# A neural codec's encoder and quantizer on one core: four residual buffers with shared code columns, exponentials in dead buffers, strict silu phases, and a fixed list that orders all operations

## The chip, the core and the metric

The kernel runs on one core of one Trainium2 chip. Five engines work side by side, each through its own stream of instructions, and wait for one another by semaphores: TensorE (PE; its weight loads are listed apart as PEld), VectorE (DVE), ScalarE (ACT), GpSimd (POOL) and SyncE (SP, which here only issues DMAs). The metric is device time in microseconds, the median of the runs. Beside it stands one profiled execution, from which every duration below is taken.

## The reference

`x` is 2 x 16000 x 512 in bf16. A depthwise convolution over time with three taps, a silu, four rounds of residual vector quantization with eight code words each, and a second depthwise convolution of the summed code words:

```python
xp = jnp.pad(x, ((0,0),(pad,pad),(0,0)))
z = jnp.zeros_like(x)
for i in range(K):                       # K = 3
    z = z + xp[:, i:i+T, :] * dw_enc[i][None, None, :]
z = _silu(z)
res = z
q = jnp.zeros_like(z)
for s in range(Nq):                      # Nq = 4, C = 8 words each
    cb = codebooks[s]
    d2 = (res . res)[..., None] - 2.0 * (res . cb) + (cb . cb)[None, None, :]   # in bf16
    idx = d2.argmin(-1)
    sel = cb[idx]
    q = q + sel
    res = res - sel
...                                      # y: q convolved with dw_dec, three taps
```

## The kernel before, in words

Time is cut into 250 groups of 128 time steps (one per partition), and these into 17 chunks of 4, 12, 14 times 16, and 10 groups. A chunk passes through three parts.

- *Front* (`load`, `front`). DMA transposes bring `x` into `XT`, channels on partitions. For each of four blocks of 128 channels (`block(i)`): three products on DVE with the taps (`product`, L486, into a Z and two T buffers), two additions (`total`; by DMA with accumulation, L497, issued from POOL, or on DVE, L500/L502, the last one into the residual buffer RES), then silu as exponential on ACT (L508, into an E buffer), plus one on DVE (L512), reciprocal on ACT (L184), and a product on DVE (`silu`, L518). Exponential and reciprocal need different tables on ACT, and a change of table is an `ACT_TABLE_LOAD`.
- *Four rounds* (`stage`). `score` (L584, L590): PE multiplies each 64-step half of a group with itself and with the code words; the code words stand as extra columns inside RES. `lone` (ACT, L601) keeps the diagonal, `dots` (DVE, L620) copies the code columns, `total` (PE, L604, L611) adds the diagonal to them, `sums` (DVE, L616) brings the result to SBUF as VT. POOL then does `ties` (L645, L647), `distance` (L658) and `key` (L662), DVE the minimum (L666) and the one-hot (L672), POOL a copy of that (`note`, L678). PE and ACT turn the one-hot into a selection (L715 to L737), PE multiplies it with pairs of code words (L749), and DVE subtracts them from RES (`update`, L755, four per round; it reads PSUM). After the fourth round there is no update.
- *Decoder* (`finish`, `outputs`). PE multiplies the one-hots with tap-weighted code words (L773), ACT copies them to YSB (L779), SP stores them.

The rounds of one chunk are a chain across PE, ACT, DVE and POOL, so chunks are worked on side by side. There are three RES buffers, taken at a chunk's first write to RES and given back after its last scoring, four Z, four T and four E buffers, and four PSUM tiles of two banks. `Plan` collects all operations as tasks with an engine, a hold, a delay, needs, buffers and a due time (a table `START` by chunk plus `OFF` by operation). When the program is built, `Plan.run` plays this through and on each engine emits the ready task with the earliest due time. Where PE would stand idle in that play, it emits dummy matmuls (`warm`, L387; 129 in all). The order on each engine is fixed from then on; on the chip only the semaphores act.

Of the kernel before, what the change touches and what calls it, by code (L numbers as in the profile page):

```python
# [20 lines left out]
LC = 16  # L21
ROOM = 2 * GC + 2

SIZES = [4, 12] + [16] * 14 + [10]
# [5 lines left out]
WARM = 0.4  # L30
SPLIT = (1, 1, 1, 2)
RELU = (0, 1, 2, 3)

ZB, TB, EB, YB = 4, 4, 4, 2
# [3 lines left out]
START = [-49.78, -21.21, -11.1, 40.29, 77.41, 126.87, 171, 213.64, 259.89, 295.9, 339.35, 382.88, 414.63, 449.59, 490.48, 512.46, 542.77]  # L38
OFF = {
    "words": -209.08, "codes": -112.52, "col0": -187, "sums": -87.73, "mask": -228.88, "norms": -202.91, "col1": 18.74,  # L40
# [19 lines left out]
}  # L60


class Plan:

    def __init__(self, slots):
        self.slots = dict(slots)
        self.tasks = []
        self.names = []
        self.idle = None

    def add(self, engine, hold, delay, needs, due, emit, take=(), give=(), use=1.0):
        self.names.append(due)
        due = START[due[0]] + OFF[due[1]]
        self.tasks.append((engine, hold, delay, [n for n in needs if n is not None], due, emit, take, give, use))
        return len(self.tasks) - 1

    def run(self):
        tasks = self.tasks
        left = [len(t[3]) for t in tasks]
        after = [[] for _ in tasks]  # L80
        for n, t in enumerate(tasks):
            for d in t[3]:
                after[d].append(n)
        engines = list(dict.fromkeys(t[0] for t in tasks))
        ready = {e: [] for e in engines}
        until = {e: 0.0 for e in engines}
        spans = []
        for n, t in enumerate(tasks):
            if not left[n]:
                heapq.heappush(ready[t[0]], (t[4], n))  # L90
        now, events, order = 0.0, [], []
        while len(order) < len(tasks):
            going = True
            while going:
                going = False
                for e in engines:
                    if until[e] > now + 1e-9:
                        continue
                    passed, pick = [], None
# [46 lines left out]
def kernel(  # L146
# [235 lines left out]
    def warm():  # L382
        if not scored[2:]:
            return False
# [488 lines left out]
```

## Time and profile before

| what | value |
|---|---|
| median of 3 runs | 815.28 us (812.22 to 817.3) |
| profiled execution, its own time | 809.59 us |
| its span, first to last instruction | 807.8 us |
| mean granted TensorE clock | 0.897 |
| DMA: moved, mean rate | 107.71 MB, 133 GB/s |

The span is what the trace covers; the time holds a little more. A view of groups has one row for each line, engine, operation and shape: number, busy time and mean duration, then the idle time of the engine just before such instructions and what ended most of it. Busy times join overlapping instructions; single durations overlap somewhat with the next one's. A view of stretches gives, for each stretch of the span, the busy time of PE, PEld, DVE, ACT and POOL (with the number of instructions), the granted clock, the busy share of the DMA engines and GB/s. A view of waits gives engine and line, what it waited for, the time in total, how often and the longest. The view of one line gives minimum, median and maximum of its durations in ns. The chain of waits follows the work that ended last back to the start.

### The profile page before, as it was taken

How to read it: one execution, taken by the hardware profiler on the slowest of the kernel's cores; microseconds unless marked ns; L12 is line 12 of the kernel's file. 1: busy time of each engine (PE TensorE's matmuls, PEld its weight loads, DVE VectorE, ACT ScalarE, POOL GpSimd, SP SyncE). 2: the span in 40 equal slices, each digit the busy share in tenths (PEclk: the TensorE clock that was granted, in tenths of full speed). 3: DMA queues.
4: the chain of work that ended last, by engine and by line, in shares of the span. 5: the costliest groups of instructions: out<-in, count | busy, mean ns of one | idle time of the engine just before them, and what ended most of it. 6: DMA issues, size and time to landing. Idle time of an engine off the chain costs nothing.

```text
span 807.8 us, 28980 instructions
## 1 busy us (share of the span) xinstructions
PE 622.8 (77%) x13019; PEld 381.0 (47%) x13092; DVE 628.2 (78%) x1027; ACT 538.6 (67%) x571; POOL 284.9 (35%) x459
## 2 busy tenths in 40 slices
PE   3065787877878878887799877878885759889985
PEld 3023454544444544535356545554553526446543
DVE  5998889896988798878778897887969785855530
ACT  2345748494789477697847976866937596793553
POOL 1244353442534155426243452253414342212200
PEclk9568788999989999989999998998998979989989
DMA  4749677767796777895967778768984542121231
GB/s 150 112 83 153 130 133 134 124 121 164 141 207 147 164 145 175 136 176 117 166 153 121 203 139 184 128 140 153 187 158 68 105 121 93 47 92 44 80 157 79
DMA packets 149542, 107.71 MB, mean 133 GB/s; under 512 B 130217, under 2 KB 131370, under 8 KB 149290
## 3 DMA queue, kind: packets, MB, share of 16 engines
q1 hardware_dynamic: 137796, 66.62, 37.4%
q0 software_dynamic: 11472, 39.10, 27.0%
q8 instruction: 102, 1.67, 0.9%
q14 instruction: 22, 0.18, 0.1%
q10 hardware_dynamic: 150, 0.13, 0.1%
HBM read 3.70 MB, written 32.77 MB: 45 GB/s over the span
## 4 chain that ended last, share of the span: by engine, by line
PE 28%; DVE 19%; ACT 14%; issue 8%; POOL 7%; DMA 3%; ACTq 0%; another core or an unknown queue 0%; DVEq 0%; POOLq 0%
PE PS L590 12%; DVE RES L755 10%; PE PS L749 5%; ACT YSB L779 4%; PE PS L584 4%; ACT E L184 3%; PE PS L773 3%; PE PS L611 2%; ACT E L508 2%; POOL S L645 2%; ACT L L601 2%; POOL D L658 2%; DVE RES L500 2%; DMA out_dram<-YSB 2%; DVE T L486 1%
## 5 line engine op out<-in xcount | busy, mean ns | idle before, releaser
L755 DVE TENSOR_TENSOR RES<-RES,PS 128x2048 bf16<-128x2048 bf16 (+2 forms) x204 | 224.5, 1136 | 26.0 <-PE PS L749 25.6
L590 PE MATMUL PS<-RES 128*64 128x80 bf16 (+1 forms) x8064 | 204.2, 208 | 36.7 <-DVE RES L518 26.7
L590 PEld LDWEIGHTS <-RES 128*64 128x64 bf16 x8064 | 170.1, 118 | 93.9 <-issue 31.7
L601 ACT ACTIVATE L<-PS 128x512 bf16<-128x512 f32 (+2 forms) x132 | 75.8, 577 | 168.5 <-PE PS L590 90.4
L749 PE MATMUL PS<-POH,PAIR 64*128 64x512 bf16 (+2 forms) x1224 | 158.4, 396 | 33.6 <-DVE RES L755 14.6
L779 ACT ACTIVATE YSB<-PS 128x1024 bf16<-128x1024 f32 (+1 forms) x126 | 124.6, 1019 | 15.3 <-PE PS L773 8.9
L184 ACT ACTIVATE E<-E 128x2048 bf16<-128x2048 bf16 (+2 forms) x68 | 120.5, 1786 | 6.6 <-DVE E L512 6.4
L658 POOL TENSOR_TENSOR D<-VT,GPOS 128x128 bf16<-128x128 bf16 (+2 forms) x68 | 45.9, 675 | 204.1 <-DVE VT L616 204.0
L749 PEld LDWEIGHTS <-PAIR 64*128 64x128 bf16 x1224 | 61.9, 102 | 103.5 <-issue 61.4
L497 POOL DMA_DIRECT2D Z<-T x75 | 73.0, 1012 | 102.7 <-issue 28.1
L508 ACT ACTIVATE E<-RES 128x2048 bf16<-128x2048 bf16 (+2 forms) x53 | 92.3, 1755 | 15.1 <-DVE RES L500 12.7
L486 DVE TENSOR_SCALAR T<-XT,WENC 128x2048 bf16<-128x2048 bf16 (+2 forms) x136 | 98.8, 739 | 3.4 <-DMA Z<-T 3.4
L773 PE MATMUL PS<-A,OHT 128*128 128x512 bf16 x224 | 80.9, 398 | 23.6 <-ACT OHT L707 5.9
L584 PE MATMUL PS<-MASK,IDENT 128*128 128x256 bf16 (+2 forms) x264 | 76.1, 288 | 12.1 <-DVE RES L755 6.0
L678 POOL COPY OH<-OH 128x128 bf16<-128x128 bf16 (+2 forms) x68 | 37.8, 562 | 121.8 <-DVE OH L672 121.7
L620 DVE CAST PR<-PS 128x64 bf16<-128x64 f32 (+2 forms) x132 | 28.8, 220 | 65.2 <-PE PS L590 50.5
L518 DVE TENSOR_TENSOR RES<-RES,E 128x2048 bf16<-128x2048 bf16 (+2 forms) x53 | 59.0, 1123 | 8.7 <-ACT E L184 8.7
L645 POOL TENSOR_SCALAR S<-VT,GMIN 128x16 f32<-128x16 bf16 (+2 forms) x68 | 51.4, 755 | 34.6 <-DVE VT L616 34.3
L500 DVE TENSOR_TENSOR RES<-Z,T 128x2048 bf16<-128x2048 bf16 (+2 forms) x53 | 63.4, 1203 | 0.1
L773 PEld LDWEIGHTS <-OHT 128*128 128x128 bf16 x373 | 32.6, 101 | 63.4 <-issue 30.2
L486 DVE TENSOR_SCALAR Z<-XT,WENC 128x2048 bf16<-128x2048 bf16 (+2 forms) x68 | 50.1, 744 | 0.2
L611 PEld LDWEIGHTS <-L 64*64 64x64 bf16 x2016 | 38.2, 111 | 20.9 <-issue 14.3
(103 smaller groups left out, 676.3 us busy)
## 6 DMA issues: line engine op xcount, KB each, us to landing
Z<-T POOLq DMA_DIRECT2D x70, 512.0 KB, 6.0
out_dram<-YSB SPq DMA_DIRECT2D x61, 512.0 KB
XT<-in_x_dram SPq DMA_TRANSPOSE x233
Z<-T POOLq DMA_DIRECT2D x5, 384.0 KB, 5.1
RES<-in_x_dram SPq DMA_DIRECT2D x1, 1536.0 KB
YSB<-in_codebooks_dram SPq DMA_DIRECT2D x12, 64.0 KB
RES<-in_x_dram SPq DMA_DIRECT2D x1, 640.0 KB
out_dram<-YSB SPq DMA_DIRECT2D x1, 384.0 KB
```

The source lines that it names most:

```text
L184: nc.scalar.add_instruction(mybir.InstActivation(name=nc.get_next_instruction_name(), engine=mybir.EngineType.Activation, ins=args, outs=[ ...
L486: nc.vector.tensor_scalar(out=u[name][:, 0:G, :], in0=XT[:, i, at + k:at + k + G, :], scalar1=WENC[:, i, k:k + 1], scalar2=None, op0=ALU.mult)
L497: nc.gpsimd.dma_start(out=z, in_=t, accum_op=ALU.add)
L500: nc.vector.tensor_tensor(out=u["R"], in0=halves(u["Z"]), in1=halves(u["ZTU"[k]]), op=ALU.add)
L508: nc.scalar.activation(halves(u["E"]), halves(u["Z"]) if adds == 2 else u["R"], ACT.Exp, scale=-1.0)
L584: nc.tensor.matmul(V[:, b, :, own:own + HT], lhsT=IDENT, rhs=MASK[:, 0:m // 2, :], start=True, stop=False, skip_group_check=True)
L590: nc.tensor.matmul(V[h * HT:(h + 1) * HT, b, r, :], lhsT=half[:, LC:LC + HT], rhs=half[:, lo:hi], start=False, stop=(i == KT - 1), skip_gr ...
L601: nc.scalar.activation(u["L", q][:, 0:m, :].rearrange("p (b r) t -> p b r t", b=2), u["V", q][:, :, :, own:own + HT], ACT.Relu)
L749: nc.tensor.matmul(u["SEL", i][:, h, 0:H * HT], lhsT=PAIR[s][rows, part, i * P:(i + 1) * P], rhs=u["POH"][rows, 0:H, :], start=(part == 0) ...
L755: nc.vector.tensor_tensor(out=tokens, in0=tokens, in1=words, op=ALU.add)
L773: nc.tensor.matmul(Y[:, h, :], lhsT=lhs(), rhs=rhs, start=(a == 0), stop=(a == len(terms) - 1))
L779: nc.scalar.activation(u["YSB"][:, k:k + n, :], u[k][:, 0:n, :], ACT.Copy)
```

## The change

- The code columns between two neighbouring halves are shared: RES holds per half 64 steps and 16 code columns (80 columns instead of 96), with the words of rounds 0 and 1 ahead of even halves and those of rounds 2 and 3 ahead of odd ones. A half reads the code columns on its left or on its right. This makes room for a fourth RES buffer.
- The exponential is written into the block's Z buffer, which is dead by then; the E buffers go, and there are seven Z buffers.
- The exponentials of a chunk wait for all reciprocals of the chunk before, its reciprocals for all its own exponentials.
- In all blocks of later chunks one of two additions is by DMA (before: one in three blocks, both in the fourth). In the full chunks the third product of blocks 2 and 3 runs on POOL.
- The `dots` of rounds 0 and 2 run on ACT. They copy five columns of groups instead of four per bank, to have the neighbour's code columns.
- The code norm's minimum stands in the last column of the PR tiles from the start, so the addition of L645 goes. The code columns, parts of the pair words and some setup move from DVE to ACT or POOL; the four PSUM tiles are cleared by DVE at the start.
- The dummy matmuls are switched off (`WARM = 0.0`).
- `Plan.run` no longer chooses: a list of 3375 numbers, `ORDER`, gives the order in which all tasks are emitted; buffers are chosen by a play of the holds.

```diff
-SIZES = [4, 12] + [16] * 14 + [10]
+SIZES = (4, 12) + (16,) * 14 + (10,)
-WARM = 0.4
-SPLIT = (1, 1, 1, 2)
-RELU = (0, 1, 2, 3)
-ZB, TB, EB, YB = 4, 4, 4, 2
+WARM = 0.0
+SPLIT = ((0, 0, 0, 0), (0, 0, 0, 0), (1, 1, 1, 1), (1, 1, 1, 1))
+POOLED = ((0, 0, 0, 0), (0, 0, 0, 0), (0, 0, 1, 1), (0, 0, 0, 0))
+CASTS = (True,False,True,False)
+SUMS = (False,) * 4
+PSB, ZB, TB, YB, LB, POHB, RESN = 4, 7, 4, 2, 2, 2, 4
...
-START = [-49.78, -21.21, -11.1, 40.29, 77.41, 126.87, 171, 213.64, 259.89, 295.9, 339.35, 382.88, 414.63, 449.59, 490.48, 512.46, 542.77]
...
+ORDER = """
+0 40 349 351 8 353 350 352 354 14 15 179 9 355 356 357 358 359 360 361 362 363 364 365 366 367 369 371 373 375 368 43 44 6 1 7 47 48 3 41 45 42 46 71
...
+        order = [int(n) for n in ORDER.split()]
+        for n in order:
+            engine, hold, delay, needs, _, emit, take, give, use = self.tasks[n]
+            begin = max([until.get(engine, 0.0)] + [end[d] for d in needs])
+            for k in take:
+                at, self.held[n, k] = free[k].pop(min(range(len(free[k])), key=lambda j: free[k][j][0]))
+                begin = max(begin, at)
...
+        t = const.tile([P, KT, 2 * GC * WD + LC], BF16, name=f"RES{n}")
...
+        pairs = t[:, :, 0:2 * GC * WD].rearrange("p k (g w) -> p k g w", w=2 * WD)
+        nc.scalar.activation(pairs[:, :, :, 0:LC], CBT[:, :, :, 0:LC].to_broadcast([P, KT, GC, LC]), ACT.Copy)
+        nc.scalar.activation(pairs[:, :, :, WD:WD + LC], CBT[:, :, :, LC:].to_broadcast([P, KT, GC, LC]), ACT.Copy)
...
+                (nc.gpsimd if k == 2 and pooled else nc.vector).tensor_scalar(out=plan.held[u[k], "Z" if k == 0 else "T"][:, 0:G, :], in0=XT[:, i, at + k:at + k + G, :],
+                                        scalar1=WENC[:, i, k:k + 1], scalar2=None, op0=ALU.mult)
...
+            def e():
+                return plan.held[u[2], "T"] if adds == 2 else z()
...
+                nc.scalar.activation(halves(e()), halves(z()) if adds == 2 else residual(), ACT.Exp, scale=-1.0)
...
-            e = plan.add("ACT", act(1.8) + load, act(1.8) + load + 0.15, [z] + turned[-1:] + st["first"], (n, f"e{i}"), exp, take=("E",))
+            x = plan.add("ACT", act(1.82) + load, act(1.82) + load + 0.13, [a] + before, (n, f"e{i}"), exp)
...
-                e = plan.add("ACT", act(1.8) + load, act(1.8) + load + 0.15, [o, ended[-1]], (n, f"v{i}"), inverse)
+                v = plan.add("ACT", act(1.82) + load, act(1.82) + load + 0.13, [o] + ended, (n, f"v{i}"), inverse)
...
+        before = turned.get(n - 1, [])
...
+                            lo, hi = (at, WD) if left(h) else (LC, WD + at + C)
...
+            src = banked(q, m // 2 + 1)[:, :, :, at:at + C]
+            dst = held(first, f"PR{s}")[:, q // m, :, 0:m // 2 + 1, 0:C]
+            if CASTS[s]:
+                nc.scalar.activation(dst, src, ACT.Copy)
+            else:
+                nc.vector.tensor_copy(dst, src)
...
         def ties():
-            u["S"] = small.tile([P, GC], F32, name="S")
-            nc.gpsimd.tensor_scalar(out=u["S"][:, 0:G], in0=u["TR"][:, 0:G], scalar1=GMIN[:, s:s + 1], scalar2=None, op0=ALU.add)
...
+            nc.gpsimd.tensor_tensor(out=u["KEY"][:, 0:G, :], in0=u["VT"][:, 0:G, C:].to_broadcast([P, G, C]),
+                                    in1=STEP.rearrange("p (o c) -> p o c", o=1).to_broadcast([P, G, C]), op=ALU.mult)
```

Lines after the change: the product is L549, the DMA addition L561, the additions on DVE L563 and L565, the exponential L571, plus one L574, silu L580, reciprocal L231, `lone` L670, `dots` L677 (ACT) and L679 (DVE), `sums` L706, the POOL steps L711 to L719, minimum L723, one-hot L726, `note` L733, `update` L818, output copy L846.

How the list moves instructions is shown at three places. First DVE in the middle of the program, around chunk 6 after its first round. Before: from its last update (RES0) to its next dots (PR0).

```order
L755 TENSOR_TENSOR RES0_103<-RES0_103,PS_5849 128x32x64
L486 TENSOR_SCALAR Z_5904<-XT_102,WENC_95 128x2048
L616 CAST VT_5976<-PS_5773 128x144
L486 TENSOR_SCALAR T2_5980<-XT_102,WENC_95 128x2048
L518 TENSOR_TENSOR RES1_104<-Z_4762,E_5687 128x32x64
L620 CAST PR0_119<-PS_5909 128x8x8
```

The same piece now, where chunk 6 has RES2 and its dots go to PR1:

```order
L818 TENSOR_TENSOR RES2_139<-RES2_139,PS0_90 128x32x64
L723 TENSOR_REDUCE M_5399<-KEY_5355 128x16
L818 TENSOR_TENSOR RES1_138<-RES1_138,PS2_92 128x32x64
L706 CAST VT_5402<-PS1_91 128x144
L726 TENSOR_TENSOR OH12_131<-KEY_5355,M_5399 128x2x8x8
L818 TENSOR_TENSOR RES1_138<-RES1_138,PS3_93 128x32x64
L549 TENSOR_SCALAR T0_110<-XT_136,WENC_89 128x2048
L549 TENSOR_SCALAR Z0_103<-XT_136,WENC_89 128x2048
L723 TENSOR_REDUCE M_5414<-KEY_5405 128x16
L679 CAST PR1_123<-PS0_90 128x10x8
```

Between update and dots stood four instructions of three chunks; now there are eight, of chunks 4, 5, 7 and 9.

Second, DVE near the end, where the last chunk (shapes with 24 or 1536) first writes to RES. Before:

```order
L672 TENSOR_TENSOR OH_14671<-T,M 128x2x8x8
L620 CAST PR_121<-PS 128x8x8 x2
L500 TENSOR_TENSOR RES_104<-Z,T_13844 128x24x64
L755 TENSOR_TENSOR RES_103<-RES_103,PS 128x32x64
L500 TENSOR_TENSOR RES_104<-Z,T_14358 128x24x64
L755 TENSOR_TENSOR RES_103<-RES_103,PS 128x32x64
```

Now:

```order
L679 CAST PR_125<-PS_91 128x10x8
L563 TENSOR_TENSOR RES_137<-Z_106,T_111 128x24x64
L818 TENSOR_TENSOR RES_138<-RES_138,PS_90 128x32x64
L706 CAST VT<-PS_91 128x144
L563 TENSOR_TENSOR RES_137<-Z_104,T_113 128x24x64
L818 TENSOR_TENSOR RES_138<-RES_138,PS_93 128x32x64
L549 TENSOR_SCALAR T_110<-XT,WENC 128x1536
```

Before, it takes the buffer of chunk 13 behind that chunk's last dots; now that of chunk 12. From the last chunk's last silu to the end, DVE has 24 updates and 7 rounds of sums, minimum and one-hot before, 32 and 11 now.

Third, POOL in the middle. Before, from one note (OH) to the next round's steps:

```order
L678 COPY OH_123<-OH_5579 128x16x8
L497 DMA Z<-T_5122 128x2048
L645 TENSOR_SCALAR S<-VT,GMIN 128x16
L647 TENSOR_TENSOR T<-S,STEP 128x128
L662 TENSOR_TENSOR T<-D_5584,T 128x128
L497 DMA Z<-T_5616 128x2048
```

Now, with a product of a front (L549) between key and note:

```order
L719 TENSOR_TENSOR KEY<-D_4430,KEY 128x128
L549 TENSOR_SCALAR T_110<-XT,WENC 128x2048
L561 DMA Z_109<-T_111 128x2048
L561 DMA Z_106<-T_113 128x2048
L733 COPY OH_127<-OH_129 128x16x8
L715 TENSOR_TENSOR KEY<-VT,STEP 128x128
```

The product stands ahead of two issues of DMA additions and the next note; L645 is gone.

More of the change, by code (lines that the diff above doesn't have):

```diff
@@ L69, in __init__, with add @@
         self.idle = None
[L71 to L74, printed above, removed]
+    def add(self, engine, hold, delay, needs, name, emit, take=(), give=(), use=1.0):
+        self.names.append(name)
+        self.tasks.append((engine, hold, delay, [n for n in needs if n is not None], name, emit, take, give, use))
@@ new lines, in add_up @@
+                if first:
+                    st["RES"] = t
+                return t
+            hold, delay = dve(0.66), dve(0.66) + 0.1
+            for k in range(2):
+                u[k] = plan.add("DVE", hold, delay, st["loaded"], (n, f"{'ztu'[k]}{i}"), lambda k=k: product(k), take=("ZT"[k],))
+            a = add_up(1, [u[0], u[1]])
+            u[2] = plan.add("POOL" if pooled else "DVE", 0.1 + 2.2 * f if pooled else hold, 0.2 + 2.2 * f if pooled else delay, st["loaded"] + [u[1]], (n, f"u{i}"),
+                            lambda: product(2), take=("T",))
@@ new lines, in stage @@
+        if s == Nq - 1:
+            plan.add("FREE", 0.0, 0.0, seen, (n, f"P{s}"), None, give=((st["RES"], "RES"),))
+        last = u["S", parts[-1][0]]
+        t = plan.add("PE", 0.16 + 0.038 * G, 0.3 + 0.038 * G, read + scored[1:], (n, f"T{s}"), total)
+        v = plan.add("ACT" if SUMS[s] else "DVE", 0.22, 0.34, [t], (n, f"V{s}"), sums,
+                     give=((last, "ps"), (u[first], f"PR{s}"), (u[first], "L")))
+        t = plan.add("POOL", 0.42, 0.5, [v], (n, f"D{s}"), distance)
+        k = plan.add("POOL", 0.48, 0.55, [v], (n, f"E{s}"), ties)
@@ L761, in stage @@
+            new.append(plan.add("DVE", 0.07 + 1.06 * f, 0.17 + 1.06 * f, [c] + seen, (n, f"U{s}{i}"), lambda i=i: update(i), give=((c, "ps"),)))
+        plan.add("FREE", 0.0, 0.0, [u["X", i] for i in range(KT)], (n, f"P{s}"), None, give=((t, "POH"),))
         st["new"] = new
-    kept = {}
     def outputs(groups, needs, n, m):
```

629 lines of the change are left out of this document (285 added, 344 removed), and 124 rows, old and new, of tables (OFF, ORDER).

## The prediction

> **What bounds the kernel now.** I read the page first: the busy totals and the shares of the chain that ended last.
>
> ```profile
> PE 622.8 (77%) x13019; PEld 381.0 (47%) x13092; DVE 628.2 (78%) x1027; ACT 538.6 (67%) x571; POOL 284.9 (35%) x459
> PE 28%; DVE 19%; ACT 14%; issue 8%; POOL 7%; DMA 3%; ACTq 0%; another core or an unknown queue 0%; DVEq 0%; POOLq 0%
> ```
>
> No engine is full and the chain is shared out, so this is a kernel of several nearly full engines that hand work round in a ring. VectorE (DVE) and TensorE (PE) carry most, and DVE is on every round trip. I therefore keep the books in DVE time: its work plus its idle time is the span. Second view, stretches of time; the cuts are the fill, the middle, the last silu of the last chunk, and the end.
>
> ```profile
> 0.00:80.00 80.00, 32.29 (x365) 19.94 (x368) 67.53 (x162) 30.92 (x32) 26.53 (x51) 0.75 0.65 126
> 80.00:680.00 600.00, 480.61 (x10481) 295.88 (x10537) 499.93 (x758) 434.45 (x442) 236.08 (x347) 0.91 0.75 145
> 680.00:724.00 44.00, 38.47 (x865) 23.55 (x869) 27.30 (x47) 33.62 (x39) 10.05 (x26) 0.92 0.21 71
> 724.00:808.00 84.00, 71.47 (x1311) 41.60 (x1318) 33.47 (x62) 39.65 (x59) 12.21 (x36) 0.94 0.22 89
> ...
> 722.81 0.96 DVE L518 TENSOR_TENSOR RES<-RES,E 128x1536 bf16<-128x1536 bf16 x1 [0.69 <-ACT E L184]
> ```
>
> The columns are PE, weight loads, DVE, ACT and POOL busy, then granted clock, DMA share and GB/s. DVE is idle 12 us in the first 80, 100 us in the middle, 17 us up to 724 and 50 us in the last 84. From 723.8 (the row of L518, the silu of the last chunk) nothing is left to fill in between, and the span is the last chunk's four rounds in series. So 808 = 595 us of DVE work ahead of that silu + 12 + 117 us of idle time + 84 us of ending.
>
> Third, who DVE waits for:
>
> ```profile
> DVE PR L620 <- PE PS L590: 50.5, 39, 2.7
> DVE M L666 <- POOL T L662: 26.6, 27, 1.8
> DVE RES L755 <- PE PS L749: 25.6, 24, 5.7
> DVE VT L616 <- PE PS L611: 21.2, 22, 2.0
> DVE PR L620 <- ACT L L601: 14.1, 17, 2.2
> DVE RES L518 <- ACT E L184: 12.5, 12, 2.4
> ```
>
> All are steps inside a round, and 64.6 us of them stand ahead of one cheap copy, the dots of L620. They are short and many: DVE arrives a little early because too little other work stands between a step and its answer. Behind that is a shortage of residual buffers:
>
> ```profile
> 643.70 0.61 DVE L486 TENSOR_SCALAR Z<-XT,WENC 128x1536 bf16<-128x1536 bf16 x1
> ...
> 695.29 0.23 DVE L620 CAST PR<-PS 128x64 bf16<-128x64 f32 x1 [1.99 <-PE PS L590]
> 695.43 0.95 DVE L500 TENSOR_TENSOR RES<-Z,T 128x1536 bf16<-128x1536 bf16 x1
> ```
>
> The last chunk's first product starts at 643.7; its first write to a residual buffer comes 52 us later, right behind the last dots of the chunk whose buffer it takes.
>
> **The change part by part.** Durations overlap by some 0.08 us on DVE, so I cost an instruction by its pace in the chain of waits: 1.13 us for an update or add, 0.66 for a product. The rows of groups give counts and the smaller prices.
>
> ```profile
> 295.24 3.39 DVE RES L755 x3
> 628.65 1.32 DVE T L486 x2
> ...
> L620 DVE CAST PR<-PS 128x64 bf16<-128x64 f32 x112 | 24.8, 223 | 53.4 <-PE PS L590 42.8 <-ACT L L601 10.1
> L250 DVE COPY RES<-CBT 128x2048 bf16<-128x2048 bf16 x3 | 3.1, 1039 | 0.0
> L249 DVE COPY RES<-CBT 128x2048 bf16<-128x2048 bf16 x3 | 2.3, 778 | 0.0
> L616 DVE CAST VT<-PS 128x144 bf16<-128x144 f32 x56 | 16.9, 302 | 17.0 <-PE PS L611 16.9
> ```
>
> *DVE's work.* Two of twelve products of each of the 14 full chunks go to POOL: 28 x 0.66 = -18.5. The dots of two rounds in four go to ACT: 66 x 0.14 = -9.2. The second add of the fourth block returns from DMA to DVE: 14 x 1.13 + 0.9 = +16.7. The code columns go to ACT: -5.4. Other setup moves (pair words, row copies, memsets of PSUM) are below 3 us each, in both directions; I take zero. Sum -16.4, so 628.2 becomes 611.8.
>
> *Where it stands.* Behind the last silu the new order has 32 updates where the old has 24, and 11 rounds of sums, minimum and one-hot instead of 7: 8 x 1.13 + 4 x 0.63 (0.22 for the sums, by L616's row less the overlap; the other two about as much) = 11.5. So 33.5 + 11.5 = 45 us of DVE work lie in the ending, and 611.8 - 45 = 567 ahead of it, against 595.
>
> *The products on POOL.* No product runs on POOL today. The nearest row is its copy of half the size:
>
> ```profile
> L444 POOL COPY XT<-XT x7: 1027/1037/2072, 54.4 to 551.5; 128x1024 bf16<-128x1024 bf16 x7
> ...
> 287.31 1.03 POOL L444 COPY XT<-XT 128x1024 bf16<-128x1024 bf16 x1
> 287.60 1.83 DVE L500 TENSOR_TENSOR RES<-Z,T 128x2048 bf16<-128x2048 bf16 x1
> ...
> L500 DVE TENSOR_TENSOR RES<-Z,T x53: 408/1217/2280, 26.9 to 706.4; 128x2048 bf16<-128x2048 bf16 x42, 128x1536 bf16<-128x1536 bf16 x7, 128x512 bf16<-128x512 bf16 x4
> L755 DVE TENSOR_TENSOR RES<-RES,PS x204: 402/1214/1223, 61.3 to 786.2; 128x2048 bf16<-128x2048 bf16 x84, 128x1536 bf16<-128x1536 bf16 x12, 128x512 bf16<-128x512 bf16 x6
> ```
>
> At 287.6 the add ran 0.6 us beyond its median: it stood until the POOL copy was through. L755, which reads PSUM, never does (its maximum is 1.223). Twice the copy is 2.05 us, so one POOL product costs DVE between 0 (updates stand beside it) and 2.05 us (an add or product comes next): 0 to 57 us for 28. In the new order sometimes four updates follow such a product, sometimes a silu or a product. I take 1 us each, +28, between the ends because about half of DVE's work reads SBUF alone.
>
> The Trainium skill ("SBUF — State Buffer", section "Who interferes with whom") says that only who issues first decides, and that the other blocks for the whole instruction. By that rule alone the price would be the upper end, 57 us, wherever the next DVE instruction uses the shared ports, and the rows above agree in kind.
>
> *POOL itself* loses the addition of L645, 15 DMA issues, and gains 28 products.
>
> ```profile
> L645 POOL TENSOR_SCALAR S<-VT,GMIN x68: 294/536/2358, 52.4 to 792.6; 128x16 f32<-128x16 bf16 x56, 128x12 f32<-128x12 bf16 x8, 128x4 f32<-128x4 bf16 x4
> L497 POOL DMA_DIRECT2D Z<-T x75 | 73.0, 1012 | 102.7 <-issue 28.1 <-DVE T L486 26.5 <-DVE PR L620 19.5
> ```
>
> That is -51 - 15 + 57, no net load at 35% busy. L645 stood in every round; its going shortens a round by about 0.5 us. But D, key and note of other chunks now queue behind a 2 us product; the larger spacing below has to hide that, and where it doesn't, the stall is the idle term again.
>
> *ACT.* Strict phases leave 33 table loads of the 47 around exponentials and reciprocals, but dots arrive.
>
> ```profile
> L184 ACT ACT_TABLE_LOAD x24 | 30.8, 1283 | 0.4
> L508 ACT ACT_TABLE_LOAD x23 | 29.5, 1283 | 11.5 <-DVE RES L500 11.1
> L720 ACT ACTIVATE OHT<-PS 128x128 bf16<-128x128 f32 x42 | 11.5, 274 | 9.5 <-PE PS L715 9.4
> ```
>
> 14 x 1.28 = -18 and 66 x 0.27 = +18, and about 10 us of columns in the fill. ACT was 72% busy in the middle; I cost it at nothing, its cover being that slack. If it is gone, the 18 us of dots are the price. Exponentials written into dead Z buffers cost no instruction; seven Z buffers instead of four Z and four E hold the fronts. The added wait is that of a chunk's first exponential for the last reciprocal of the chunk before; behind it on ACT stand relus and output copies, for whose PSUM buffers PE waits. The new order puts 13 us of DVE work between a block's last add and its "plus one", where 7 stood, so I expect the wait to have ended before it is reached.
>
> *Idle time.* Of 117 us, the dots' waits are 64.6; two rounds in four leave DVE, -32. The rest, 85, shrinks with spacing. I counted DVE work between fixed points of a chunk in both orders by the paces above: from the first round's sums to the last's, 74 us before and 85 now; from the last silu to the first sums, 9 and 18; a residual buffer is held over 113 and 147. One seventh more work between rounds takes about 13 off. So 72. The ends are 117 (spacing buys nothing) and 40: in its best stretch DVE was busy 37.1 us of 40, and 7% of some 640 us ahead of the ending is about that.
>
> ```profile
> 440.00:480.00 40.00, 31.60 (x783) 20.84 (x785) 37.12 (x57) 33.53 (x35) 17.72 (x27) 0.96 0.72 162
> ```
>
> *The ending.* Last chunk alone: 84 less 4 x 0.5 for L645. But PE was busy 71.5 of 84 there, and more rounds of other chunks now lie in it; 80 to 100, taken as 86.
>
> *Sum:* 567 + 28 + 12 + 72 + 86 = 765 us of span, 5.3% less than 807.8. The profiled execution took 809.6 for that span and the median of the three runs is 815.3, so times are 1.009 spans: **772 us**. Its own range, with POOL's price from 10 to 45, idle from 50 to 95 and the ending from 80 to 92: 719 to 811 of span, 726 to 818 us.
>
> **The rivals.** A measurement of this kernel tells about 1% from no change.
>
> 1. *DVE is kept full.* Four chunks in flight leave 40 us of idle time, and updates stand beside most POOL products (10 us): 567 + 10 + 12 + 40 + 84 = 713, or 720 us. For it: 147 against 113 us of cover. Against: PE was itself busy 480.6 of 600.
> 2. *The shared ports decide: slower.* Every POOL product blocks DVE for its full length, the round's POOL steps queue behind it, and spacing is used up: 567 + 57 + 12 + 117 + 88 = 841, or 849 us. The switch is at about 1 us per product if no idle time is won (567 + 28 + 12 + 117 + 86 = 810). For it the row of 287.6; against, that updates are immune and that there are few large steps on POOL.
> 3. *The order buys nothing.* That last sum, 817 us: the waits only move to ACT and PE.
> 4. *TensorE's clock.* The change drops the dummy multiplications that filled PE's gaps.
>
> ```profile
> 40.00:80.00 40.00, 14.78 (x44) 5.04 (x47) 0.76 0.71 119
> 160.00:200.00 40.00, 0.38 (x1) 0.10 (x1) 0.97 0.75 147
> sum 800.00, PE 38.65 PEld 11.85; mean PE 1.93 PEld 0.59
> ```
>
> These rows, of line L387 by stretches of 40 us, put 14.8 of 38.7 us into the fill, where the clock is 0.76 even so; at 160 to 200 there is one and the clock is 0.97. So I expect no loss in the middle. If the clock fell there from 0.91 to 0.78, PE's 28% of the chain, 226 us, would grow by a sixth, +38: 803, or 810 us.
>
> The Trainium skill ("TensorE: Matmul & The Clock Gate", Part 1) says that an idle window throttles the array and sustained work releases it. By that rule dropping the fillers speaks against this change, with the time of rival 4, unless real work fills the windows, as the row of 160 to 200 suggests.
>
> **How the numbers follow.** Forecast 0.55; rivals 1 to 4: 0.15, 0.12, 0.10, 0.08. The range of 718 to 828 us leaves out half of rival 1 and nearly all of rival 2. Faster by over 1% (below 807): 0.53 + 0.15 + 0.03 of rival 3 + 0.02 of rival 4 = 0.73. Within 1%: 0.02 + 0.05 + 0.03 = 0.10. Slower: 0.12 + 0.02 + 0.03 = 0.17.
>
> **What would show it.** DVE busy near 612 to 640 us (the excess is blocking, to be seen as adds and products beyond 1.22 and 0.75 us beside POOL's product, with updates at 1.21); DVE's idle in the middle below 75 us, dots' waits halved; 33 table loads apart from the first; the last silu some 85 us ahead of the end; the clock in the middle at 0.9. It is wrong if DVE's products and adds grow by more than 60 us in sum, if the waits at L706, L723 and L818 grow instead of shrinking, or if the clock falls below 0.8.

## The result and the profile after

| | before | after |
|---|---|---|
| median | 815.89 us (6 runs, 812.22 to 818.97) | 822.56 us (6 runs, 820.15 to 823.83) |
| profiled span | 807.8 us | 818.0 us |
| mean granted clock | 0.897 | 0.859 |

The ratio of after to before is 1.0081, 95% interval 1.0051 to 1.0110. The kernel got slower by a little, under 1%, where 772 us was forecast. The time lies inside the wide range of 718 to 828 us, but beyond the 726 to 818 us of the sum itself, and on the wrong side of the kernel before.

First the page of after: the busy totals (busy time, share of the span, instructions).

```profile
PE 607.1 (74%) x13031; PEld 376.4 (46%) x13031; DVE 692.0 (85%) x919; ACT 544.9 (67%) x640; POOL 400.4 (49%) x411
```

DVE has 108 instructions fewer than before and is busy 64 us longer. POOL gained 115 us. Next the view of stretches, with the cuts at the same places as before: the fill, the middle, the last silu of the last chunk (it ends at 717.0), and the end. The columns are as before.

```profile
0.00:80.00 80.00, 18.65 (x314) 15.57 (x314) 65.83 (x120) 41.98 (x47) 33.20 (x45) 0.67 0.62 126
80.00:673.00 593.00, 456.47 (x9753) 281.14 (x9755) 542.98 (x666) 410.87 (x462) 340.38 (x301) 0.85 0.68 132
673.00:717.00 44.00, 42.41 (x1062) 26.27 (x1058) 37.99 (x56) 38.88 (x48) 11.23 (x22) 1.00 0.16 48
717.00:818.00 101.00, 89.56 (x1906) 53.38 (x1904) 45.22 (x80) 53.17 (x84) 15.62 (x45) 0.99 0.24 96
```

In the prediction's own books (DVE's work ahead of the last silu, its idle time there, the ending), the DVE column of the first three rows adds up to 646.8 us, and 717.0 less that is the idle time:

| us | before | forecast | after |
|---|---|---|---|
| DVE's work ahead of the last silu | 595 | 595 (567 + 28) | 646.8 |
| DVE's idle time ahead of it | 129 | 84 | 70.2 |
| ending | 84 | 86 | 101.0 |
| span | 808 | 765 | 818.0 |

So the idle time went, by more than forecast, and DVE's work came in its place. The groups of DVE's instructions show which work grew (count, busy time, mean duration in ns, idle time before).

```profile
L818 DVE TENSOR_TENSOR RES<-RES,PS 128x2048 bf16<-128x2048 bf16 x168 | 200.1, 1213 | 21.8 <-PE PS L812 19.0 <-ACT Y L846 1.0 <-ACT PR L677 0.5
L549 DVE TENSOR_SCALAR T<-XT,WENC 128x2048 bf16<-128x2048 bf16 x84 | 86.0, 1030 | 0.2
L580 DVE TENSOR_TENSOR RES<-RES,Z 128x2048 bf16<-128x2048 bf16 x56 | 83.5, 1497 | 4.1 <-ACT Z L231 4.1
L563 DVE TENSOR_TENSOR RES<-Z,T 128x2048 bf16<-128x2048 bf16 x56 | 82.6, 1486 | 0.6 <-PE PS L666 0.6
L549 DVE TENSOR_SCALAR Z<-XT,WENC 128x2048 bf16<-128x2048 bf16 x56 | 67.5, 1211 | 0.3
L726 DVE TENSOR_TENSOR OH<-KEY,M 128x128 bf16<-128x128 f32 x56 | 23.8, 427 | 0.7
```

The same groups before:

```profile
L755 DVE TENSOR_TENSOR RES<-RES,PS 128x2048 bf16<-128x2048 bf16 x168 | 198.1, 1214 | 17.6 <-PE PS L749 17.1
L486 DVE TENSOR_SCALAR T<-XT,WENC 128x2048 bf16<-128x2048 bf16 x112 | 85.7, 777 | 3.4 <-DMA Z<-T 3.4
L518 DVE TENSOR_TENSOR RES<-RES,E 128x2048 bf16<-128x2048 bf16 x42 | 50.7, 1218 | 6.6 <-ACT E L184 6.6
L500 DVE TENSOR_TENSOR RES<-Z,T 128x2048 bf16<-128x2048 bf16 x42 | 54.5, 1304 | 0.1
L486 DVE TENSOR_SCALAR Z<-XT,WENC 128x2048 bf16<-128x2048 bf16 x56 | 42.9, 771 | 0.2
L672 DVE TENSOR_TENSOR OH<-T,M 128x128 bf16<-128x128 f32 x56 | 16.1, 291 | 0.4
```

The updates (L818, which read PSUM) stand at 1213 ns as ever. The products rose from 777 and 771 to 1030 and 1211 ns, the adds (L563) from 1304 to 1486, the silus (L580) from 1218 to 1497 and the one-hots (L726) from 291 to 427. By these means the products grew by 46 us in sum, the adds by 10, the silus by 16 and the one-hots by 8. The cause stands in POOL's group of the moved products.

```profile
L549 POOL TENSOR_SCALAR T<-XT,WENC 128x2048 bf16<-128x2048 bf16 x28 | 163.7, 5852 | 9.0 <-DMA Z<-T 4.6 <-DVE RES L563 4.2
```

One product takes 5.85 us on POOL, where the prediction had bounded it by 2.05. The timelines of DVE and POOL around 354 and 557 us (start, duration, engine) show what DVE does meanwhile.

```profile
353.87 5.43 POOL L549 TENSOR_SCALAR T<-XT,WENC 128x2048 bf16<-128x2048 bf16 x1
354.48 5.38 DVE L549 TENSOR_SCALAR T<-XT,WENC 128x2048 bf16<-128x2048 bf16 x1
...
557.28 6.42 DVE L549 TENSOR_SCALAR Z<-XT,WENC 128x2048 bf16<-128x2048 bf16 x1
557.52 5.62 POOL L549 TENSOR_SCALAR T<-XT,WENC 128x2048 bf16<-128x2048 bf16 x1
563.62 0.27 DVE L723 TENSOR_REDUCE M<-KEY 128x16 f32<-128x128 f32 x1
```

Both products of DVE, otherwise 0.75 us long, are through 0.56 us after POOL's (359.86 against 359.30, 563.70 against 563.14). They stood for nearly all of it. The profile books such standing as busy time: DVE's 85% hold some 80 us in which it did nothing. Last, whom DVE waits for by its semaphores (time in total, times, longest).

```profile
DVE RES L818 <- PE PS L812: 27.4, 27, 3.2
DVE PR L679 <- ACT L L670: 23.2, 17, 6.3
DVE M L723 <- POOL KEY L719: 19.9, 23, 1.5
DVE VT L706 <- PE PS L697: 12.8, 15, 3.2
DVE PR L679 <- PE PS L666: 4.4, 3, 3.4
```

The dots' waits fell from 64.6 to 27.6 us, those of the sums from 21.2 to 12.8.

### The profile page after: what moved, and what is told of

Read it like the earlier page. It is cut to its first block, busy times and chain, and to the rows that moved or that the text cites. A ratio compares the mean times of both kernels' runs of the same rounds, so it can differ in the third digit from the quotient of the medians.

```text
span 818.0 us, 29058 instructions
## 1 busy us (share of the span) xinstructions
PE 607.1 (74%) x13031; PEld 376.4 (46%) x13031; DVE 692.0 (85%) x919; ACT 544.9 (67%) x640; POOL 400.4 (49%) x411
## 5 line engine op out<-in xcount | busy, mean ns | idle before, releaser
L818 DVE TENSOR_TENSOR RES<-RES,PS 128x2048 bf16<-128x2048 bf16 (+2 forms) x204 | 227.0, 1134 | 30.3 <-PE PS L812 27.4
L666 PE MATMUL PS<-RES 128*64 128x72 bf16 (+1 forms) x8064 | 212.5, 209 | 40.7 <-DVE RES L580 35.0
L549 POOL TENSOR_SCALAR T<-XT,WENC 128x2048 bf16<-128x2048 bf16 x28 | 163.7, 5852 | 9.0 <-DMA Z<-T 4.6
L846 ACT ACTIVATE Y<-PS 128x1024 bf16<-128x1024 f32 (+1 forms) x126 | 125.0, 1015 | 50.3 <-PE PS L842 42.0
L571 ACT ACTIVATE Z<-RES 128x2048 bf16<-128x2048 bf16 (+2 forms) x68 | 119.7, 1784 | 23.8 <-DVE RES L563 23.5
L670 ACT ACTIVATE L<-PS 128x512 bf16<-128x512 f32 (+2 forms) x132 | 74.6, 578 | 78.1 <-DVE PR L679 44.1
L231 ACT ACTIVATE Z<-Z 128x2048 bf16<-128x2048 bf16 (+2 forms) x68 | 119.4, 1781 | 3.0 <-DVE Z L574 2.8
L561 POOL DMA_DIRECT2D Z<-T x60 | 56.7, 965 | 105.6 <-issue 22.1
L842 PE MATMUL PS<-A,FIN 128*128 128x512 bf16 x249 | 90.2, 408 | 14.7 <-DVE RES L818 5.9
L549 DVE TENSOR_SCALAR T<-XT,WENC 128x2048 bf16<-128x2048 bf16 (+2 forms) x108 | 99.3, 929 | 0.2
L580 DVE TENSOR_TENSOR RES<-RES,Z 128x2048 bf16<-128x2048 bf16 (+2 forms) x68 | 92.7, 1370 | 4.2 <-ACT Z L231 4.1
L563 DVE TENSOR_TENSOR RES<-Z,T 128x2048 bf16<-128x2048 bf16 (+2 forms) x68 | 92.5, 1373 | 0.7 <-PE PS L666 0.6
L711 POOL TENSOR_TENSOR D<-VT,GPOS 128x128 bf16<-128x128 bf16 (+2 forms) x68 | 44.5, 665 | 97.7 <-DVE VT L706 97.7
L715 POOL TENSOR_TENSOR KEY<-VT,STEP 128x128 f32<-128x128 bf16 (+2 forms) x68 | 43.0, 632 | 83.2 <-DVE VT L706 83.1
L733 POOL COPY OH<-OH 128x128 bf16<-128x128 bf16 (+2 forms) x68 | 47.8, 716 | 71.8 <-DVE OH L726 66.8
L549 DVE TENSOR_SCALAR Z<-XT,WENC 128x2048 bf16<-128x2048 bf16 (+2 forms) x68 | 74.5, 1103 | 0.5 <-ACT XT L472 0.2
L842 PEld LDWEIGHTS <-FIN 128*128 128x128 bf16 x373 | 31.5, 102 | 62.9 <-issue 38.1
L782 PE MATMUL PS<-TWO,OH 128*128 128x128 bf16 (+2 forms) x51 | 12.1, 242 | 55.5 <-DVE OH L726 52.6
```

The source lines that it names most:

```text
L231: nc.scalar.add_instruction(mybir.InstActivation(name=nc.get_next_instruction_name(), engine=mybir.EngineType.Activation, ins=args, outs=[ ...
L549: (nc.gpsimd if k == 2 and pooled else nc.vector).tensor_scalar(out=plan.held[u[k], "Z" if k == 0 else "T"][:, 0:G, :], in0=XT[:, i, at + ...
L563: nc.vector.tensor_tensor(out=residual(), in0=halves(z()), in1=halves(t), op=ALU.add)
L571: nc.scalar.activation(halves(e()), halves(z()) if adds == 2 else residual(), ACT.Exp, scale=-1.0)
L580: nc.vector.tensor_tensor(out=residual(), in0=halves(z()) if adds == 2 else residual(), in1=halves(e()), op=ALU.mult)
L666: nc.tensor.matmul(V[h * HT:(h + 1) * HT, b, r * WD + lo:r * WD + hi], lhsT=RES[:, i, own + LC:own + WD], rhs=RES[:, i, own + lo:own + hi] ...
```

## The experiments

Medians of 4 runs unless another number is given. Ratios are to the kernel before, run on the same chip (814.1 to 816.7 us).

**1. All products back on DVE.** Theory A: POOL's products are the whole loss. Rival B: the lost clock of TensorE is.

```diff
-POOLED = ((0, 0, 0, 0), (0, 0, 0, 0), (0, 0, 1, 1), (0, 0, 0, 0))
+POOLED = ((0, 0, 0, 0), (0, 0, 0, 0), (0, 0, 0, 0), (0, 0, 0, 0))
```

> All third products are on DVE again; everything else, the list included, is as in the changed kernel. Theory A (POOL's 28 products, 5.85 us each, make DVE stand: in the changed trace the adds, products, silus and one-hots that run beside POOL take about 92 us more than alone): DVE busy falls from 692 to about 630 us (minus 92, plus 28 x 0.66, plus some 12 us of the small blocking that the kernel before shows too), idle time ahead of the last silu grows from 68 by 0 to 30 us, time 762 to 796 us. Rival B (TensorE's clock, 0.54 from 40 to 120 us, and TensorE's work set the time): 805 us or more, DVE's idle time up by what its busy time fell. Rival C (the list was made for products on POOL, the gain is given back as waits): 812 to 825 us, idle ahead of the last silu 120 us or more.

Measured: 759.02 us, ratio 0.9288 [0.9224, 0.9352]. The page's totals and the view of stretches, cut at its last silu (656.9):

```profile
PE 589.0 (78%) x13031; PEld 366.9 (48%) x13031; DVE 628.8 (83%) x947; ACT 543.6 (72%) x640; POOL 242.7 (32%) x383
...
0.00:80.00 80.00, 17.43 (x314) 14.40 (x314) 65.39 (x130) 44.97 (x51) 23.34 (x47) 0.67 0.66 130
80.00:613.00 533.00, 440.15 (x9757) 272.94 (x9758) 480.29 (x684) 406.69 (x459) 192.51 (x270) 0.90 0.78 146
613.00:657.00 44.00, 41.89 (x1059) 26.15 (x1057) 38.03 (x56) 38.82 (x48) 11.28 (x22) 1.00 0.15 48
657.00:758.00 101.00, 89.50 (x1906) 53.40 (x1904) 45.12 (x79) 53.17 (x84) 15.57 (x45) 0.98 0.25 96
```

DVE has 28 instructions more than after and is busy 63 us less. In the books: 583.7 of work, 73.3 idle, 101.0 of ending. This one line turns a small loss into the fastest kernel of the study, and the clock in its middle stretch is 0.90 without a dummy multiplication. Theory A holds, with a time 3 us below its range; rival B had 805 us or more and rival C 812 or more.

**2. A copy on POOL in the product's place.** The third tap's factor is left out in these blocks.

```diff
-                (nc.gpsimd if k == 2 and pooled else nc.vector).tensor_scalar(out=plan.held[u[k], "Z" if k == 0 else "T"][:, 0:G, :], in0=XT[:, i, at + k:at + k + G, :],
+                if k == 2 and pooled:
+                    nc.gpsimd.tensor_copy(plan.held[u[k], "T"][:, 0:G, :], XT[:, i, at + k:at + k + G, :])
+                    return
+                nc.vector.tensor_scalar(out=plan.held[u[k], "Z" if k == 0 else "T"][:, 0:G, :], in0=XT[:, i, at + k:at + k + G, :],
```

> The 28 third products on POOL become plain copies on POOL of the same size (the tap's factor is left out in these blocks, so the output differs). It tests the price that the prediction used, 2.05 us for an instruction on POOL. Theory A: the copy takes 2.0 to 2.5 us, DVE's excess beside it is near 28 us plus the small blocking, DVE busy 635 to 655 us, time 765 to 800 us, near the prediction of 772. Rival A2 (what counts is the traffic through the shared ports, not how long POOL's instruction lasts): the copy too is stretched to 4 us or more and the time stays above 805. Rival B: no change, 815 to 825.

Measured: 761.58 us, ratio 0.9336 [0.9281, 0.9391]. The view of groups, and the busy totals:

```profile
L550 POOL COPY T<-XT 128x2048 bf16<-128x2048 bf16 x28 | 58.3, 2091 | 12.5 <-DVE RES L566 6.9 <-DMA Z<-T 5.6
...
PE 591.2 (77%) x13031; PEld 369.8 (48%) x13031; DVE 634.5 (83%) x919; ACT 544.2 (71%) x640; POOL 292.6 (38%) x411
```

The copy takes what the prediction took for the product (2.09 us), and the time comes within 1.4% of the forecast. Theory A holds; its ranges (635 us of DVE, 765 us) were missed by 0.5 and 3.4 us on the fast side. It is not the place of the instruction but its length that lost the time.

**3 and 4. The dummy multiplications on again**, with POOL's products (3) and without them (4).

```diff
-WARM = 0.0
+WARM = 0.4
```

> The changed kernel with the dummy matmuls switched on as before (0.4). Theory A: the granted clock from 40 to 120 us rises from 0.54 to about 0.75 and the mean from 0.86 to about 0.89, but DVE is 37 to 40 us busy of each 40 us there, so the time falls by 0 to 10 us: 812 to 823. Rival B: the slow TensorE in the fill is what costs, the time falls by 25 us or more, below 798.

> Products on DVE and dummy matmuls on. Theory A: as products on DVE alone less 0 to 15 us (with DVE less loaded, TensorE's clock in the fill is worth more): 750 to 792 us. Rival B: the dummies bring the larger part of the difference. Rival C: 805 or more.

Measured: 824.24 us, ratio 1.0108 [1.0051, 1.0165], and 762.44 us, ratio 0.9307 [0.9233, 0.9380]. The stretch from 40 to 120 us of after, of experiment 3, of experiment 1 and of experiment 4, in this order:

```profile
40.00:120.00 80.00, 27.63 (x499) 20.31 (x501) 76.20 (x102) 52.43 (x55) 47.66 (x34) 0.54 0.60 108
...
40.00:120.00 80.00, 42.32 (x521) 24.20 (x522) 75.55 (x101) 51.44 (x55) 47.53 (x32) 0.57 0.59 107
...
40.00:120.00 80.00, 37.82 (x687) 27.53 (x689) 74.27 (x122) 57.39 (x66) 31.53 (x38) 0.54 0.72 127
...
40.00:120.00 80.00, 44.36 (x725) 28.63 (x727) 73.36 (x122) 57.11 (x66) 33.15 (x38) 0.69 0.68 126
```

Before had 0.78 there. With POOL's products the dummies hardly raised the clock there (0.54 to 0.57, where about 0.75 was expected), so experiment 3, just above theory A's 812 to 823 us, says little; why they did not is open. In the pair 1 and 4 the clock of the fill rises from 0.54 to 0.69 and the time does not fall. Rival B is out: the clock fell, as rival 4 of the prediction said, but most of all in a stretch where DVE is busy 73 to 76 of 80 us and PE has slack.

**5. POOL's product in two halves**, the question being whether DVE gets in between two instructions.

```diff
+                if k == 2 and pooled:
+                    for lo, hi in ((0, G // 2), (G // 2, G)):
+                        nc.gpsimd.tensor_scalar(out=plan.held[u[k], "T"][:, lo:hi, :], in0=XT[:, i, at + k + lo:at + k + hi, :],
+                                                scalar1=WENC[:, i, k:k + 1], scalar2=None, op0=ALU.mult)
+                    return
...
```

> The changed kernel with each of the 28 products on POOL issued as two instructions of 1024 elements per partition; nothing else differs and the output is unchanged. Theory A1 (the port is held per instruction): each half takes some 2.7 us, POOL's total for them stays near 160 us, but VectorE gets in between the halves, so its excess beside POOL's products falls from about 92 us to 50 to 75 and the time to 785 to 812 us. Rival A2 (what counts is the total time POOL works on SBUF, VectorE waits through both halves): excess 80 to 95 us, time 815 to 828 us.

Measured: 796.23 us, ratio 0.9736 [0.9698, 0.9775]. Theory A1 holds in its mechanism and its time; the standing fell further than the 50 to 75 us that it said, to about 25 (the table below). DVE's idle time ahead of the last silu rose from 70 to 99 us.

**6. A constant factor.** As after, but POOL multiplies by 0.05 instead of the tap of each partition; the third tap's factor is left out in these blocks.

```diff
+                if k == 2 and pooled:
+                    nc.gpsimd.tensor_scalar(out=plan.held[u[k], "T"][:, 0:G, :], in0=XT[:, i, at + k:at + k + G, :],
+                                            scalar1=0.05, scalar2=None, op0=ALU.mult)
+                    return
...
```

> The changed kernel with the 28 products on POOL by an immediate factor 0.05 in place of the tap of each partition; so the third tap's own factor is left out in these blocks. Theory A3 (the per-partition operand makes POOL's product slow): the product takes about 2.05 us as the copy does, and the time is 755 to 775 us. Rival A4 (multiplying on POOL is slow as such, with whatever factor): 5.4 to 5.9 us a product, and 812 to 828 us.

Measured (10 runs): 817.93 us, ratio 1.0010 [0.9981, 1.0039]. The one line of this product in the trace (minimum, median, maximum in ns):

```profile
L550 POOL TENSOR_SCALAR T<-XT x28: 5354/5404/6846, 64.3 to 646.6; 128x2048 bf16<-128x2048 bf16 x28
```

Rival A4 holds: the multiplication is slow on POOL with either factor, at least 5.35 us where the copy of the same size took 1.88 at least.

**7. All dots on DVE**, on top of experiment 1.

```diff
-CASTS = (True,False,True,False)
+CASTS = (False,False,False,False)
```

> The first experiment's kernel (all products on VectorE, 759.0 us) with the dots of all four rounds on VectorE, in the same order. Theory C (the dots on ScalarE are worth what the prediction put on them, 9 us of VectorE's work and some 32 us of its idle time): time 775 to 805 us, idle time ahead of the last silu 90 to 115 us where it was 73. Rival D (spacing alone took the dots' waits away, ScalarE only costs a little less work): time 757 to 770 us, idle time below 80 us.

Measured: 807.55 us, ratio 0.9866 [0.9833, 0.9898]. DVE's idle time ahead of the last silu is 112.4 us where it was 73.3, its work 593.7 where it was 583.7. Whom DVE waits for:

```profile
DVE PR L679 <- ACT L L670: 40.2, 32, 5.7
DVE RES L818 <- PE PS L812: 33.0, 33, 3.3
DVE VT L706 <- PE PS L697: 25.4, 24, 2.5
DVE PR L679 <- PE PS L666: 18.9, 13, 3.0
```

Theory C holds, at the upper end and 2.5 us beyond it: 59.1 us of waits ahead of the dots, with the longer spacing in place. So the spacing alone did not take these waits away. Moving half of the dots to ACT did, and is worth 48.5 us with this list, more than what the kernel gains on the one before without it (9 us). The list was made for dots on ACT; what one made for dots on DVE would take was not tried.

**8. Three residual buffers**, on top of experiment 1. The list is kept; a task that finds no free buffer is put off until there is one.

```diff
-PSB, ZB, TB, YB, LB, POHB, RESN = 4, 7, 4, 2, 2, 2, 4
+PSB, ZB, TB, YB, LB, POHB, RESN = 4, 7, 4, 2, 2, 2, 3
...
-        for n in order:
+        for n in turns():
```

> The first experiment's kernel (all products on VectorE, 759.0 us) with three residual buffers in place of four; the list is kept, except that a task that finds no free buffer is put off until one is given back. Theory E (the fourth buffer gives the spacing that took the idle time away): idle time ahead of the last silu rises from 73 to 110 us or more, time 785 to 830 us. Rival F (the order alone does it, the fourth buffer is not needed): idle time below 85 us, time below 772 us.

Measured: 1018.03 us, ratio 1.2451 [1.2397, 1.2505]; idle time 313.6 us. It is far beyond theory E's figure, probably because every postponed task drags along what needs it, on all engines; that was not taken apart. It shows that this list does not stand without the fourth buffer. What a list made for three buffers would take stays open.

**9. POOL's product in eight pieces.** As experiment 5, with eighths.

```diff
-                    for lo, hi in ((0, G // 2), (G // 2, G)):
+                    for lo, hi in [(j * G // 8, (j + 1) * G // 8) for j in range(8)]:
```

> The changed kernel with each of the 28 products on POOL issued as eight instructions of 256 elements per partition; the output is unchanged. With two halves VectorE's excess was 26 us where it is 82 with whole products, and its idle time ahead of the last silu 99 us where it is 70. Theory A1 (the port is held per instruction, the gap between two of them lets VectorE through): the excess stays below 40 us, POOL's total for the products stays below 200 us, and the time is 785 to 815 us, still 25 to 55 us above the kernel with all products on VectorE (759.0 us), because POOL is busy longer. Rival A5 (each boundary hands the port back and forth and each piece costs VectorE its own block): the excess is back at 60 us or more and the time above 815 us.

Measured: 847.89 us, ratio 1.0414 [1.0332, 1.0496]. DVE's standing fell as A1 said, but POOL's time for the products rose to 260 us, beyond its figure of 200, and with it the time left its range; A5 had the time, but not the cause, since the standing did not come back. Two lines of DVE's waits:

```profile
DVE M L728 <- POOL KEY L724: 64.2, 26, 9.0
DVE RES L568 <- POOL T L551: 46.4, 10, 10.6
```

In after the first was 19.9 us and the second did not occur. What DVE no longer stands, it waits, for the round's key and for the product itself.

**10 and 11. The products on ACT**: both blocks (10), block 3 alone (11), on top of experiment 1.

```diff
+                if k == 2 and sort == 2 and i in (2, 3):
+                    nc.scalar.activation(plan.held[u[k], "T"][:, 0:G, :], XT[:, i, at + k:at + k + G, :], ACT.Copy, scale=WENC[:, i, k:k + 1])
+                    return
...
```

> The first experiment's kernel (759.0 us) with the 28 third products of blocks 2 and 3 as scaled copies on ScalarE in place of VectorE, in the same order; the output keeps its meaning. Theory G (VectorE's work is what counts, ScalarE at 72% has room): 18.5 us less work on VectorE, some 28 x 1.9 = 53 us more on ScalarE, time 738 to 755 us. Rival H (ScalarE is on the rounds' path, and what stands behind a 2 us product there is late): VectorE's idle time grows by more than its work falls, time 762 to 800 us.

> As the one before, but only the 14 third products of block 3 on ScalarE: 9.2 us less work on VectorE, some 27 us more on ScalarE. Theory G: time 747 to 756 us. Rival H: 760 to 780 us.

Measured: 779.78 us, ratio 0.9554 [0.9483, 0.9625], and 763.92 us, ratio 0.9379 [0.9311, 0.9448]. Of experiment 10 the totals, ACT's group of the products and DVE's longest wait:

```profile
PE 594.4 (76%) x13031; PEld 369.7 (48%) x13031; DVE 612.1 (79%) x919; ACT 594.8 (76%) x668; POOL 238.0 (31%) x383
...
L550 ACT ACTIVATE T<-XT,WENC 128x2048 bf16<-128x2048 bf16 x28 | 55.5, 2001 | 1.0 <-DVE RES L566 1.0
...
DVE RES L821 <- PE PS L815: 48.3, 38, 5.8
```

Rival H holds for both. In experiment 10 DVE's work falls by 16.7 us and its idle time ahead of the last silu rises from 73.3 to 110.3; the updates' wait for PE, whose selections come by way of ACT, went from 27.7 to 48.3. Neither beats experiment 1; experiment 11 can't be told from it, since the intervals overlap. Here too the list is the one made for other places.

**The products in one table.** Experiment 10 has DVE's 919 instructions of after and no product on POOL, so DVE's busy time beyond its 612.1 us is taken as the time it stood for POOL; the share is that of POOL's time. For after, the means of DVE's groups give the same by another way: against experiment 1 the products, adds, silus and one-hots of the full shape are longer by 21.2 + 23.7 + 12.9 + 14.8 + 7.7 = 80.3 us.

| the 28 products | POOL busy with them | DVE stood | share | DVE idle ahead of the last silu | time |
|---|---|---|---|---|---|
| on POOL, whole (after) | 163.7 | 79.9 | 49% | 70.2 | 822.56 |
| on POOL, constant factor | 157.8 | 69.7 | 44% | 75.1 | 817.93 |
| on POOL, copies instead | 58.3 | 22.4 | 38% | 74.1 | 761.58 |
| on POOL, two halves | 176.4 | 24.6 | 14% | 99.3 | 796.23 |
| on POOL, eight pieces | 260.3 | 9.0 | 3% | 165.4 | 847.89 |
| on ACT | 0 | 0 | | 110.3 | 779.78 |
| on DVE | 0 | (16.7 of work) | | 73.3 | 759.02 |

## Why the prediction was wrong

*The step that failed* is the price of the products on POOL, +28 us. "The nearest row is its copy of half the size … Twice the copy is 2.05 us, so one POOL product costs DVE between 0 … and 2.05 us". The share was right: 1 us of 2.05 was taken, 49%, and after shows 49% (79.9 of 163.7). That it is the same figure is partly luck, for the share hangs on the length: it is 38% with copies and 14% with halves. The duration was wrong: 5.85 us instead of 2.05. The term measures 80 instead of 28 (by the shares, 28 x 5.85 x 0.49). Put into the prediction's own sum, 567 + 80 + 12 + 72 + 86 = 817 us of span, where 818.0 were measured. Experiment 2 is the cross-check: with an instruction of the length that was assumed, the term is 22.4 and the time 761.58. Why a multiplication takes 2.8 times a copy's time on POOL stays open.

The trace of before held a better row, seen in hindsight. On POOL a copy is not the nearest relation of a product; another arithmetic operation is, and there was one on a large shape:

```profile
L343 POOL TENSOR_TENSOR PAIR<-YSB,PAIR x3: 1151/1160/1765, 17.6 to 72.3; 128x512 bf16<-128x512 f32 x3
```

For 512 elements 1.15 to 1.77 us, so four times that, 4.6 to 7.1 us, for 2048: the measured 5.4 to 7.4 lie close. That they lie so close is partly luck, since this operation has two inputs, of another type. With it the upper bound of the term would have been above 100 us and its middle above 60. The prediction went by the size, and left out that a copy does no arithmetic.

*The same step* hid a second one: "*POOL itself* … no net load at 35% busy". POOL's busy share went to 49%.

*What held.* Without the failed term the sum stands: the prediction's 567 us of work, plus 18.5 for the products back on DVE, plus 12 + 72 + 86, is 755.5 us, and experiment 1 has a span of 757.9. DVE's work is right to 2 us (585.5 and 583.7). The idle time ahead of the last silu was put at 84 and measured 73.3. The ending holds 45 us of DVE work as forecast. It lasts 101.0 instead of 86, in experiments 1 and 4 too, so it is not the doing of POOL's products. PE is busy 89.6 us in it (89.5 and 90.1 there), so the prediction seems to have given PE's work too little weight when it took 86 between ends of 80 and 100; no run tests that. These two misses, 11 and 15 us in experiment 1 and 14 and 15 in after, cancel: that the sums come within 3 us is luck.

*The dots* were costed at -9.2 us of work and -32 of idle time; experiment 7 shows 10.0 and 39.1. *ACT*: 33 table loads were forecast and counted, besides the first. It was costed at nothing with the cover of its slack; the dots there gain more than they cost (experiment 7), but experiment 10 shows how little slack is left in this list: 55.5 us more there cost 37 us of DVE's idle time.

*The rivals.* Rival 2 named the right mechanism at the wrong size: it charged the full 2.05 us, and expected the spacing to be used up, which it was not (70 us idle). By the Trainium skill ("SBUF — State Buffer", section "Who interferes with whom") the later one blocks for the whole instruction. The row of 354.48 agrees: DVE's product came 0.61 us after POOL's and lasted 5.38 us. At 557.28 DVE's record begins 0.24 us before POOL's, so that row doesn't tell which was issued first. What happens when the product is cut into pieces agrees as well. What is stated there about who contends agrees too: the updates, with one operand in PSUM, stay at 1213 ns, while the products (scalar multiplications of SBUF) and the adds, silus and one-hots, with two SBUF inputs, are lengthened. The upper end of that rule with the measured duration would have been 28 x 5.85 = 164 us; half of it came. Rival 3's time (817) came by another way; its statement, that the waits only move, is refuted by 70 us of idle time. Rival 1 is refuted by the same number, 70 where it had 52 (its 40 us for the middle were low by their own row too: 7.2% of 640 us is 46). Rival 4 saw the clock fall, most in the fill (0.54 from 40 to 120 us, 0.78 before), at no cost there: experiment 1 has the same 0.54, and raising it to 0.69 in experiment 4 won nothing. Against the forecast it also fell behind the fill, from 120 to 280 us to 0.81, where it was 0.92 before; but there experiments 1 and 4 both have 0.87, without and with the dummies. Further on it is 0.90, where before had 0.91.

*The signs.* "It is wrong if DVE's products and adds grow by more than 60 us in sum" was all but met: products and adds grew by 56 us against before and 58 against experiment 1. The sign left out the silus and one-hots; with them it is about 80. The waits at L706 and L723 shrank, from 21.2 to 12.8 and from 26.6 to 19.9; that at L818 rose a little, 25.6 to 27.4. The clock was below 0.8 in the first 160 us (0.79, 0.54, 0.54 and 0.71 in steps of 40 us) and once more from 280 to 320 us (0.79); over the whole span it was 0.859.

Of the 53 us between the forecast's span and the measured one, the products thus make 52, and the other misses cancel. That the change as a whole, less this one line, is worth 7% is shown. How the remaining gain divides among the fourth buffer, the spacing and the second additions was not taken apart, beyond the dots.

## What to carry to other kernels

When work is moved to an engine that does not do such work yet, take its price from a row that does the same sort of thing there on a large shape, not from a copy of the right size; between two candidate rows the slower one sets the upper bound. Here POOL's time on SBUF was paid twice: DVE stood for part of it as "busy" time, and what was queued on POOL came late. Cutting the instruction up exchanged the first for the second: two halves won 26 us by it, eight pieces lost 25. If an engine's instructions get longer while those that read PSUM don't, look at what POOL does at that moment before believing the engine's busy share.

## What the hardware showed beyond this

- A multiplication by a scalar on POOL costs 2.6 ns for each element of a partition (5.35 us for 2048 at least), a copy 0.92 to 1.02 (1.88 to 2.09 us), with the same types, shapes and buffers. A factor that is the same for all partitions saves 0.2 us of 5.85. The Trainium skill ("GPSIMD Engine Reference", section 4.1, "Engine selection") calls operations with one input roughly line-rate there. No run here shows what that rate is; but the copy and the multiplication by a constant both have one input, and the multiplication takes 2.8 times as long at least (5.35 against 1.88 us), so the statement can't fit both.
- Halving the instruction took DVE's standing from 79.9 to 24.6 us while POOL's own time grew by 13 us only. Pieces of an eighth had a minimum of 0.91 us, 7.3 us for all eight, but took 260 us for the 28 products, 9.3 us for each: with many boundaries it was POOL that stood. In that trace the 66 pieces that began while DVE worked on SBUF alone lasted 1.84 us on average, the other 158 only 1.03 to 1.09. Why two halves already take away two thirds of the standing, and not half, was not settled.
- The same multiplication took 2.00 us on ACT and added 0.6 us each to DVE's busy time (16.7 us for 28).
